# A radix-2 step of the transform over d, moved from TensorE to VectorE, ScalarE and GpSimd, with row- and column-tiled matmuls behind it

## The chip, the cores and the metric

One NeuronCore of a Trainium2 chip runs the whole kernel as one program. The metric is device time in microseconds (us), the median of three runs. Besides these there is one profiled execution, whose trace is the source of every duration below. Engines are named as in the profile: PE is TensorE's matmul stream and PEld its weight loads, DVE is VectorE, ACT ScalarE, POOL GpSimd, and SP is SyncE, whose queue issues all of this kernel's transfers.

## The reference

```python
x = A_x                                    # (1, 2048, 512) f32
xn = layernorm(x, axis=-1)
# A: spectral filter over both axes (S = 2048, D = 512)
X = rfft2(xn, axes=(-2, -1)) * (A_w_r + 1j * A_w_i)        # 2048 x 257
a = irfft2(X, s=(S, D), axes=(-2, -1))
# B: Dense -> Mish -> Dense, F = 1792
h = xn @ B_w1 + B_b1
b = (h * tanh(softplus(h))) @ B_w2
return x + a + b
```

Everything is f32 on input and output. On TensorE each f32 operand is written as a sum of two f16 numbers, high and low.

## The kernel before, in words

Two pieces of work share the engines. The MLP (B) is 56 tiles (4 row groups g by 14 blocks f of the hidden axis). Each tile is two half tiles: `mlp_up` (12 matmuls of 128x128 weights by 512 columns into `ph`, then Mish on ACT into `hb`, then a split of `hb` into high and low f16 halves `a`) and `mlp_down` (12 matmuls by 512 columns into `pa`). The helper `mm3` (lines 59 to 65) is the f16 pair product: high by high, high by low, low by high, three matmuls, each with its own weight load.

The spectral filter (A) is a chain of matrix products with DRAM between them, because each step needs another axis on the partitions:

- `s1_forward`, 16 units: transform over 128 values of the row axis, three matmuls of 512 columns into `psS`; ACT and DVE write the high and the low half of `y1`; two units are stored together to `d_y1`.
- `p2_unit`, 16 units (4 rounds c by 4 groups g): loads `yt` from `d_y1`; the remaining 16-point transform over rows, mixed with a radix-4 step over d; 12 matmuls with 128x128 weights (the data) and 128 moving columns (the constants) into `psP`; ACT and DVE write `z`.
- `spectrum`, 4 rounds: the rest of the transform over d. `dmm` makes the pairs `ere`/`eim` and `ore`/`oim`, each of 2 x 6 matmuls of 512 columns. DVE and POOL separate the even part into its components (`X`), multiply by the filter (tiles `wE`, `wO`, loaded in `p2_unit`), and combine (`w`, `o`). Row 0 goes a way of its own through small copies (`g0`, `r0`, `h0`). Each result is split into f16 halves in `u`.
- `dp_unit`, 16 units: inverse transform over d, 12 matmuls with weights `u` and 256 moving columns into `psA`; ACT and DVE write `at`, which is stored to `d_a`.
- `ip_unit`, 16 units: loads `ai` from `d_a`; three matmuls of 512 columns into `psT`; ACT and DVE write `tt`, stored to `d_t`.
- `s1_inverse`, 16 units: loads `yi` from `d_t`; three matmuls of 512 columns into `psY`; DVE adds the result to the MLP's output or to x.

Before them come the loading and scaling of the MLP's weights (`load_w1`, `w2_scale`, `split_w1`, `split_w2`), layernorm with transposes of the rows through TensorE (`norm`, tiles `xh`, `pt`, `xnT`), and the largest magnitude of the filter (`prep_spectral`).

The order is set at the end of the kernel function. `stream_a` is a generator over the spectral units from `p2_unit` to `ip_unit`; after each of its steps, as many half tiles of the MLP are emitted as keep pace with `B_END` = 100 of 112 half tiles over `N_UNITS` = 72 steps. The rest of the MLP is spread over the 16 `s1_inverse` units. The tile scheduler then fixes the order on each engine at build time: by priority in program order, but letting a later instruction go first where an earlier one isn't ready in its model. The first matmul of a spectral group is tied behind the previously emitted matmul (`keep_in_program_order`), so it can't move ahead of MLP work emitted before it, while later MLP work may move ahead of it. `issue_after` puts `w2_scale` behind the last DVE instruction of the first four `s1_forward` units.

Buffers that matter: the PSUM pool `ps_f` has two banks (tag "f"), used by `psS`, `psP`, the results of `dmm`, `psA`, `psT` and `psY`; `ps_h` has two, for `ph` and the transposes; `ps_a` has four, for the MLP's accumulators. In SBUF the tiles `z` and `u` have one buffer each, `at` and `tt` share three, `yt`, `ai`, `yi` and `xh` share four.

Of the kernel before, what the change touches and what calls it, by code (L numbers as in the profile page):

```python
# [19 lines left out]
P = 128  # L20
# [10 lines left out]
O_P2, O_IP2, O_DE, O_DO, O_IE, O_IO, O_ID = 0, 512, 1024, 2048, 3072, 4096, 5120  # L31
# [4 lines left out]
def spectral_mlp_kernel(ctx, tc, x, wt, w0, w1, b1, w2, cT, cIT, cM, out):  # L36
# [17 lines left out]

    d_y1 = dp.tile([64, P, 256], F16, tag="d_y1", name="d_y1")
# [15 lines left out]
    c_p2 = cMt[:, O_P2 : O_P2 + 512].rearrange("p (v h q) -> p v h q", v=2, h=2)  # L71
    c_ip2 = cMt[:, O_IP2 : O_IP2 + 512].rearrange("p (v h q) -> p v h q", v=2, h=2)
    c_de = cMt[:, O_DE : O_DE + 1024].rearrange("p (e o h q) -> p e o h q", e=2, o=2, h=2)
    c_do = cMt[:, O_DO : O_DO + 1024].rearrange("p (e o h q) -> p e o h q", e=2, o=2, h=2)
    c_ie = cMt[:, O_IE : O_IE + 1024].rearrange("p (e h q) -> p e h q", e=2, h=2)
    c_io = cMt[:, O_IO : O_IO + 1024].rearrange("p (e h q) -> p e h q", e=2, h=2)
# [14 lines left out]
    y1s = {}  # L91

    def s1_forward(g, s, xh):
        if True:
            s2 = 4 * g + s
            ps = ps_f.tile([P, D], F32, tag="f", name=f"psS1_{s2}")
            mm3(ps, lambda h: cTt[:, s2, h, :], lambda h: xh[:, h, :], True, True)
            if s % 2 == 0:
                y1s[0] = tp.tile([P, 2, 4, 2, P], F16, tag="X", name=f"y1_{s2}", bufs=2)
            y1v = y1s[0][:, s % 2]  # L100
            psv = ps.rearrange("p (a b) -> p a b", a=4)
# [4 lines left out]
            if s % 2 == 1:  # L106
                nc.sync.dma_start(
                    d_y1[4 * (s2 - 1) : 4 * (s2 + 1)].rearrange("a p e -> p a e"),
                    y1s[0].rearrange("p s a h e -> p (s a) (h e)"),
                )  # L110
        return last.ins
# [21 lines left out]
    def norm(g, ts):  # L133
# [14 lines left out]
        for s in range(4):  # L148
# [5 lines left out]
            if g == 0:  # L154
                xh = tp.tile([P, 2, D], F16, tag=f"w{s}", name=f"xh_{s2}")
            else:
                xh = qp.tile([P, 2, D], F16, tag="q1", name=f"xh_{s2}")
# [132 lines left out]
    def prep_spectral():  # L290
        mxw = sp.tile([P, 9], F32, tag="mxw", name="mxw")
        for c in range(8):
            t = big.tile([P, 1024], F32, tag="big", name=f"wm_{c}")
            nc.sync.dma_start(t, wt[:, c // 2, 1024 * (c % 2) : 1024 * (c % 2) + 1024])
            nc.vector.tensor_reduce(mxw[:, c : c + 1], t, axis=AX.X, op=ALU.max, apply_absolute_value=True)
            yield 1.1
# [11 lines left out]
        sc["u"] = scalars("u", pW, 2.0**-16, recip=True)  # L308
# [14 lines left out]
    def halves(t):  # L323
        v = t.rearrange("p (g a q) -> p a g q", g=4, a=2)
        return v[:, 0], v[:, 1]

    def flat(t):
        return t.rearrange("p a b -> p (a b)")

    zt, ut, wts = {}, {}, {}  # L330

    def p2_unit(c, g):
        if g == 0:
            wEt = big.tile([P, 2, 512], F32, tag="big", name=f"wE_{c}")
            nc.sync.dma_start(flat(wEt), wt[:, c, 0:1024])
            wOt = big.tile([P, 2, 512], F32, tag="big", name=f"wO_{c}")
            nc.sync.dma_start(flat(wOt), wt[:, c, 1024:2048])
            wts[c] = (wEt, wOt)
            zt[c] = tp.tile([P, 2, 4, 4, P], F16, tag="z", name=f"z_{c}")
        z = zt[c]  # L340
        if True:
            fg = 4 * c + g
            yt = qp.tile([P, 4, 2, P], F16, tag="q1", name=f"yt_{fg}")
            nc.sync.dma_start(
                yt.rearrange("p a h e -> p (a h e)"),
                d_y1.rearrange("a (c f) e -> (a c) (f e)", c=2)[:, fg * 1024 : (fg + 1) * 1024],
            )
            ps = ps_f.tile([P, 4, P], F32, tag="f", name=f"psP2_{fg}")
# [3 lines left out]
            psv = ps.rearrange("p l (k q) -> p k q l", k=4)  # L352
            zh = z[:, 0, :, g, :].rearrange("p k (q l) -> p k q l", l=4)
            zl = z[:, 1, :, g, :].rearrange("p k (q l) -> p k q l", l=4)
            nc.scalar.mul(zh, psv, 2.0**-14)
            nc.vector.scalar_tensor_tensor(zl, psv, 2.0**-14, zh, op0=ALU.mult, op1=ALU.subtract)

    def spectrum(c):
        s_u, c0t = sc["u"], sc["c0t"]
        z = zt[c]  # L360
        wEt, wOt = wts[c]
        u = tp.tile([P, 2, 4, 4, P], F16, tag="u", name=f"u_{c}")
        ut[c] = u

        def dmm(name, mat, k0, o):
            ps = ps_f.tile([P, 512], F32, tag="f", name=name)
            for e in range(2):
                mm3(
                    ps,
                    lambda h: mat[:, e, o, h, :],  # L370
                    lambda h: z[:, h, k0 + e].rearrange("p g q -> p (g q)"),
                    e == 0,
                    e == 1,
                    e == 0,
                )
            return ps

        def split_u(k, r):
            split(flat(u[:, 0, k]), flat(u[:, 1, k]), r, s_u)

        ere = dmm(f"ere_{c}", c_de, 0, 0)
        eim = dmm(f"eim_{c}", c_de, 0, 1)
        es = tp.tile([P, 512], F32, tag="xs", name=f"es_{c}", bufs=2)
        nc.scalar.copy(es, eim)

        er0 = tp.tile([1, 512], F32, tag="xs", name=f"er0_{c}", bufs=2)
        nc.scalar.copy(er0, ere[0:1, :])  # L387
        q0 = slice(32 * c, 32 * c + 4)
        g0 = sp.tile([P, 2, 2, 64], F32, tag="g0", name=f"g0_{c}")
        nc.sync.dma_start(  # L390
            g0[q0, 0].rearrange("g a q -> g (a q)"), er0.rearrange("p (g q) -> p g q", g=4)
        )
        nc.sync.dma_start(
            g0[q0, 1].rearrange("g a q -> g (a q)"), es[0:1].rearrange("p (g q) -> p g q", g=4)
        )
        r0 = sp.tile([P, 2, 2, 64], F32, tag="r0", name=f"r0_{c}")
        for a in range(2):
            m2 = sp.tile([P, 2, 64], F32, tag="m2", name=f"m2_{c}_{a}")
            nc.vector.tensor_mul(r0[q0, :, a, :], g0[q0, :, 0, :], c0t[q0, 2 * a])
            nc.vector.tensor_mul(m2[q0], g0[q0, :, 1, :], c0t[q0, 2 * a + 1])  # L400
            nc.vector.tensor_add(r0[q0, :, a, :], r0[q0, :, a, :], m2[q0])
# [9 lines left out]
        def xq(k):  # L411
            return X[:, k].rearrange("p (g q) -> p g q", g=4)
# [466 lines left out]
```

## Time and profile before

| | |
|---|---|
| median of 3 runs | 422.85 us (420.85 to 426.03) |
| profiled execution | 426.21 us |
| its span, first to last instruction | 424.4 us |
| mean granted TensorE clock | 0.986 of full |
| PE busy | 391.0 us, 2099 matmuls |
| DVE busy | 241.3 us, 453 instructions |
| ACT busy | 172.4 us, 261 instructions |
| POOL busy | 42.2 us, 45 instructions |
| DMA | 61.02 MB, mean 144 GB/s |

Times in the profile are those of the profiled execution. A row of a timeline gives the start and the duration in us, then engine, line of the kernel, operation, output and inputs with the buffer numbers left out, and shapes (for a matmul: weights, then moving operand); a bracket behind it is the idle time of its engine before it and what ended that. Matmul durations are modelled and overlap the next matmul; the distance from start to start is what a matmul costs in a stream. A row of a group of instructions gives total busy time and mean ns of one behind the bar, and a row for a tile gives the shortest, median and longest duration. A row of waits gives the total in us, the number of times and the longest one.

### The profile page before, as it was taken

Reading aid. Unit: us, or ns where it says so; the run is one execution under the profiler, and the core shown is the slowest. Engines: PE = TensorE matmul, PEld = TensorE weight load, DVE = VectorE, ACT = ScalarE, POOL = GpSimd, SP = SyncE. Lnnn points to the kernel's source line nnn. Section 1 sums busy time; section 2 is a strip of 40 time slices with the busy share of each in tenths; the row PEclk is TensorE's granted clock in tenths of the full one; section 3 lists DMA queues with packets and bytes.
Section 4 is the critical chain, followed back from the end, with each engine's and each line's share of the span. In section 5 each row is a group of like instructions: output and inputs, shape, how many; then the busy total and the mean of one; then the engine's idle time right before and its main releaser. Section 6 shows DMA issues by size and latency. Waiting matters only on the chain.

```text
span 424.4 us, 5542 instructions
## 1 busy us (share of the span) xinstructions
PE 391.0 (92%) x2099; PEld 194.1 (46%) x2099; DVE 241.3 (57%) x453; ACT 172.4 (41%) x261; POOL 42.2 (10%) x45
## 2 busy tenths in 40 slices
PE   0787899499899999989999999999999999999995
PEld 0433344244445455436554455554455544554442
DVE  5759899995455123773247943339625287332554
ACT  2896462442635324334343334333524243433110
POOL 0000102332040000220002020011200022000000
PEclk9999999889999999989999999999999999999999
DMA  7899882588154701032227214233024210233796
GB/s 247 268 345 330 272 259 91 159 256 269 53 160 114 233 25 51 0 99 71 81 76 239 85 49 123 76 127 124 2 74 151 74 51 25 76 127 126 219 296 247
DMA packets 48811, 61.02 MB, mean 144 GB/s; under 512 B 3168, under 2 KB 31360, under 8 KB 48528
## 3 DMA queue, kind: packets, MB, share of 16 engines
q1 hardware_dynamic: 48784, 60.67, 44.7%
q8 instruction: 16, 0.26, 0.2%
q14 instruction: 11, 0.09, 0.1%
HBM read 43.85 MB, written 16.78 MB: 143 GB/s over the span
## 4 chain that ended last, share of the span: by engine, by line
PE 72%; DVE 13%; DMA 6%; ACT 4%; issue 2%; POOL 0%; SPq 0%; DVEq 0%; ACTq 0%; POOLq 0%
PE pa L65 9%; PE pa L64 9%; PE pa L61 9%; PE ph L61 9%; PE ph L65 9%; PE ph L64 9%; DVE q L273 2%; DMA w1s<-in_w_dram 2%; PE pt L164 2%; ACT w1t L236 1%; PE psA L61 1%; PE psA L64 1%; PE psA L65 1%; DMA w2s<-in_w_dram 1%; DMA ai<-d_a 1%
## 5 line engine op out<-in xcount | busy, mean ns | idle before, releaser
L61 PE MATMUL ph<-xnT,w1t 128*128 128x512 f16 x224 | 85.2, 380 | 2.6 <-ACT hb L533 1.5
L533 ACT ACTIVATE hb<-ph,b1t,sc_exp 128x512 f32<-128x512 f32 x56 | 43.4, 775 | 107.4 <-PE ph L65 104.2
L65 PE MATMUL ph<-xnT,w1t 128*128 128x512 f16 x224 | 84.8, 379 | 2.4 <-DVE w1t L208 2.4
L61 PE MATMUL pa<-w2t,a 128*128 128x512 f16 x224 | 85.3, 383 | 1.6 <-ACT w2t L207 1.6
L64 PE MATMUL pa<-w2t,a 128*128 128x512 f16 x224 | 85.7, 383 | 0.3 <-DVE w2t L208 0.3
L65 PE MATMUL pa<-w2t,a 128*128 128x512 f16 x224 | 86.0, 384 | 0.0
L208 DVE SCALAR_TENSOR_TENSOR a<-hb,sc_a,a 128x512 f16<-128x512 f32 x56 | 42.3, 755 | 76.2 <-ACT a L207 76.1
L64 PE MATMUL ph<-xnT,w1t 128*128 128x512 f16 x224 | 85.0, 379 | 0.0
L207 ACT ACTIVATE a<-hb,sc_a 128x512 f16<-128x512 f32 x56 | 40.1, 719 | 2.2 <-PE pa L65 0.9
L65 PEld LDWEIGHTS <-w1t 128*128 128x128 f16 x224 | 21.9, 98 | 29.7 <-DVE w1t L208 3.4
L65 PEld LDWEIGHTS <-a 128*128 128x128 f16 x224 | 22.0, 98 | 27.4 <-issue 1.6
L64 PEld LDWEIGHTS <-w1t 128*128 128x128 f16 x224 | 21.9, 98 | 27.1 <-issue 2.3
L61 PEld LDWEIGHTS <-a 128*128 128x128 f16 x224 | 22.1, 99 | 26.5 <-issue 2.7
L61 PEld LDWEIGHTS <-w1t 128*128 128x128 f16 x224 | 21.9, 98 | 26.4 <-ACT w1t L207 1.6
L64 PEld LDWEIGHTS <-a 128*128 128x128 f16 x224 | 22.1, 99 | 25.2 <-issue 1.1
L164 PE MATMUL pt<-cMt,xh 128*128 128x128 f16 x128 | 12.3, 253 | 18.5 <-ACT xh L159 11.3
L487 DVE SCALAR_TENSOR_TENSOR at<-psA,at 128x512 f16<-128x512 f32 x16 | 11.0, 689 | 19.1 <-ACT at L486 19.1
L422 POOL TENSOR_TENSOR w<-X,wE 128x512 f32<-128x512 f32 x4 | 5.1, 1269 | 165.7 <-ACT er L387 76.8
L164 PEld LDWEIGHTS <-xh 128*128 128x128 f16 x128 | 10.3, 114 | 23.7 <-ACT xh L159 12.0
L509 DVE SCALAR_TENSOR_TENSOR tt<-psT,tt 128x512 f16<-128x512 f32 x16 | 11.0, 690 | 14.1 <-ACT tt L508 13.9
L160 POOL TENSOR_TENSOR xh<-xs,xh 128x512 f16<-128x512 f32 x12 | 14.4, 1216 | 45.2 <-ACT xh L159 29.9
L486 ACT ACTIVATE at<-psA 128x512 f16<-128x512 f32 x16 | 9.4, 589 | 22.8 <-PE psA L65 22.8
(150 smaller groups left out, 551.2 us busy)
## 6 DMA issues: line engine op xcount, KB each, us to landing
x<-in_x_dram SPq DMA_DIRECT2D x8, 512.0 KB
d_y<-y SPq DMA_DIRECT2D x8, 512.0 KB
wm<-in_wt_dram SPq DMA_DIRECT2D x8, 512.0 KB
yt<-d_y SPq DMA_DIRECT2D x16, 256.0 KB
d_a<-at SPq DMA_DIRECT2D x16, 256.0 KB
ai<-d_a SPq DMA_DIRECT2D x16, 256.0 KB
d_t<-tt SPq DMA_DIRECT2D x16, 256.0 KB
yi<-d_t SPq DMA_DIRECT2D x16, 256.0 KB
```

The costliest lines, as they stand in the source:

```text
L61: first = nc.tensor.matmul(ps, stat(0), mov(0), start=start, stop=False)
L64: nc.tensor.matmul(ps, stat(0), mov(1), start=False, stop=False)
L65: nc.tensor.matmul(ps, stat(1), mov(0), start=False, stop=stop)
L160: (nc.vector if g == 0 else nc.gpsimd).tensor_sub(xh[:, 1, :], xs, xh[:, 0, :])
L164: nc.tensor.transpose(pt[:, h, dc, :], xh[:, h, dc * P : (dc + 1) * P], ident)
L207: hi = nc.scalar.activation(dst_h, src, AF.Copy, scale=scale)
L208: nc.vector.scalar_tensor_tensor(dst_l, src, scale, dst_h, op0=ALU.mult, op1=ALU.subtract)
L273: nc.vector.tensor_reduce(q[:, c : c + 1], t, axis=AX.XY, op=ALU.max, apply_absolute_value=True)
L486: nc.scalar.mul(at[:, :, 0, :], ps, 2.0**-15)
L487: nc.vector.scalar_tensor_tensor(at[:, :, 1, :], ps, 2.0**-15, at[:, :, 0, :], op0=ALU.mult, op1=ALU.subtract)
L509: nc.vector.scalar_tensor_tensor(tt[:, :, 1, :], ps, 2.0**-12, tt[:, :, 0, :], op0=ALU.mult, op1=ALU.subtract)
L533: nc.scalar.activation(hb, ph, AF.Mish, bias=b1t[:, f : f + 1], scale=s_exp[k])
```

## The change

The first radix-2 step over d (rows a and a + 256 of the d axis) is done where `y1` is evicted: a new helper `butterfly` forms sum and difference of the two halves of the PSUM tile in f32, and splits the result into f16 halves with a copy on ACT and a subtraction on POOL. The same helper does the last radix-2 step of the inverse in `ip_unit`. `y1` is stored unit by unit.

The matrices behind it are halved. `p2_unit` issues 24 matmuls with 64 columns of weights, alternating between the lower and upper 64 output partitions (column tiles), so that one half of the partitions of `z` holds one half of the frequencies and the other half the rest. `d_pair` takes the place of `dmm`: 24 matmuls with 64 rows, alternating between the two halves of the rows (row tiles) into two PSUM banks. `product` takes the place of the multiplications by the filter; real and imaginary parts now lie in different partition halves. `load_wt` loads the filter inside `spectrum`, each piece twice, once for each half of the partitions. `dp_unit` keeps its 12 matmuls and moves 128 columns instead of 256; `ip_unit` has 6 matmuls of 256 columns instead of 3 of 512. `s1_inverse` reads its input in another order.

```diff
+    def butterfly(out, a, b, scale, name):
+        bc = tp.tile([P, 256], F32, tag="bc", name=f"bc_{name}", bufs=2)
+        nc.scalar.mul(bc, b, scale)
+        t = tp.tile([P, 4, 2, 64], F32, tag="bt", name=f"bt_{name}", bufs=2)
+        av = a.rearrange("p (k e) -> p k e", k=4)
+        bv = bc.rearrange("p (k e) -> p k e", k=4)
+        nc.vector.scalar_tensor_tensor(t[:, :, 0], av, scale, bv, op0=ALU.mult, op1=ALU.add)
+        last = nc.vector.scalar_tensor_tensor(t[:, :, 1], av, scale, bv, op0=ALU.mult, op1=ALU.subtract)
+        tv = t.rearrange("p k c e -> p k (c e)")
+        nc.scalar.copy(out[:, :, 0, :], tv)
+        nc.gpsimd.tensor_sub(out[:, :, 1, :], tv, out[:, :, 0, :])
+        return last.ins
...
     def s1_forward(g, s, xh):
-            nc.scalar.mul(y1v[:, :, 0, :], psv, 2.0**-17)
-            last = nc.vector.scalar_tensor_tensor(
-                y1v[:, :, 1, :], psv, 2.0**-17, y1v[:, :, 0, :], op0=ALU.mult, op1=ALU.subtract
-            )
+        y1 = tp.tile([P, 4, 2, P], F16, tag="q2", name=f"y1_{s2}", bufs=3)
+        last = butterfly(y1, ps[:, 0:256], ps[:, 256:512], 2.0**-17, f"s1_{s2}")
...
     def p2_unit(c, g):
-            for l in range(4):
-                v = 1 if fg == 0 and l == 0 else 0
-                mm3(ps[:, l, :], lambda h: yt[:, l, h, :], lambda h: c_p2[:, v, h, :], True, True, l == 0)
+        for pr in range(2):
+            for k in range(2):
+                for t, (hs, hm) in enumerate(((0, 0), (0, 1), (1, 0))):
+                    for be in range(2):
+                        v = int(fg == 0 and pr == 0 and be == 0)
+                        first = nc.tensor.matmul(
+                            ps[64 * be : 64 * be + 64, pr, k, :],
+                            yt[:, 2 * pr + be, hs, k, :],
+                            c_p2[:, k, v, hm, :],
+                            start=t == 0,
+                            stop=t == 2,
+                        )
...
+    def load_wt(c, be):
+        w = []
+        for ri in range(2):
+            t = big.tile([P, 4, 256], F32, tag="big", name=f"wt_{c}_{be}_{ri}")
+            at = 1024 * (4 * c + 2 * be + ri)
+            for h in range(2):
+                nc.sync.dma_start(t[64 * h : 64 * h + 64].rearrange("p k q -> p (k q)"), wt[:, at : at + 1024])
+            w.append(t)
+        wts[c, be] = w
...
+    def d_pair(c, k0):
+        z = zt[c]
+        ps = [ps_f.tile([P, 2, 256], F32, tag="f", name=f"psD_{c}_{k0}_{be}") for be in range(2)]
+        for k in range(2):
+            for e in range(2):
+                for t, (hs, hm) in enumerate(((0, 0), (0, 1), (1, 0))):
+                    for be in range(2):
+                        rows = slice(64 * be, 64 * be + 64)
+                        first = nc.tensor.matmul(
+                            ps[be][:, k],
+                            c_d[rows, k0 + k, e, hs, :],
+                            z[rows, hm, 2 * (k0 + k) + e].rearrange("p g q -> p (g q)"),
+                            start=e == 0 and t == 0,
+                            stop=e == 1 and t == 2,
+                        )
...
+    def product(r, x, w, k, name):
+        wre, wim = w[0][:, k], w[1][:, k]
+        t2 = tp.tile([P, 2, 256], F32, tag="t2", name=f"t2_{name}", bufs=2)[:, 0 : k.stop - k.start]
+        nc.vector.tensor_mul(r, x, wre)
+        nc.vector.scalar_tensor_tensor(
+            t2[0:64], x[64:128], -1.0, wim[64:128], op0=ALU.mult, op1=ALU.mult
+        )
+        nc.vector.tensor_mul(t2[64:128], x[0:64], wim[0:64])
+        nc.gpsimd.tensor_add(r, r, t2)
...
     def spectrum(c):
+        ab = d_pair(c, 0)
+        xa, es = [], []
+        for be in range(2):
+            load_wt(c, be)
+            e = tp.tile([P, 256], F32, tag="es", name=f"es_{c}_{be}", bufs=2)
+            nc.scalar.copy(e, ab[be][:, 0])
+            for r in range(2):
+                nc.sync.dma_start(
+                    g0[q0, r, be].rearrange("g a q -> g (a q)"),
+                    e[64 * r : 64 * r + 1].rearrange("p (g q) -> p g q", g=4),
+                )
+            ea, eb = halves(e)
+            nc.scalar.mul(jbv[0:64], eb[64:128], -1.0)
+            nc.scalar.copy(jbv[64:128], eb[0:64])
+            nc.vector.tensor_add(xp, ea, jbv)
+            nc.vector.tensor_sub(xm, ea, jbv)
...
+            yield 1.6
...
+        for be in range(2):
+            w = wts[c, be]
+            r = tp.tile([P, 2, 256], F32, tag="r", name=f"r_{c}_{be}", bufs=2)
+            product(r[:, 1:2], ab[be][:, 1:2], w, slice(1, 2), f"b_{c}_{be}")
+            ra = tp.tile([P, 1, 256], F32, tag="ra", name=f"ra_{c}_{be}", bufs=2)
+            product(ra, xa[be], w, slice(0, 1), f"a_{c}_{be}")
+            rp, rm = halves(ra[:, 0])
+            ua, ub = halves(r[:, 0])
+            nc.vector.tensor_add(ua, rp, rm)
+            nc.vector.tensor_sub(ub[0:64], rp[64:128], rm[64:128])
+            nc.vector.tensor_sub(ub[64:128], rm[0:64], rp[0:64])
...
+            split_u(0, be, r)
+            yield 2.0
...
+        cd = d_pair(c, 2)
+        for be in range(2):
+            r = tp.tile([P, 2, 256], F32, tag="r", name=f"r2_{c}_{be}", bufs=2)
+            product(r, cd[be], wts[c, be], slice(2, 4), f"c_{c}_{be}")
+            split_u(2, be, r)
+            yield 2.0
...
     def dp_unit(c, g):
-            for k, m in ((0, c_ie), (2, c_io)):
-                pk = flat(ps[:, k : k + 2])
-                for e in range(2):
-                    mm3(pk, lambda h: u[:, h, k + e, g, :], lambda h: m[:, e, h, :], e == 0, e == 1, k == 0 and e == 0)
+        for k in range(4):
+            mm3(
+                ps[:, k % 2, :, k // 2, :],
+                lambda h: u[:, h, k, g].rearrange("p q r b -> p (q r b)"),
+                lambda h: c_id[:, k, h, :].rearrange("p (e d) -> p e d", e=2),
+                True,
+                True,
+                k == 0,
+            )
...
     def ip_unit(c, g):
-                mm3(ps, lambda h: c_ip2[:, 0, h, :], lambda h: ai[:, :, h, :], True, True, True)
+        for k in range(2):
+            parts = [(1, slice(0, 1)), (0, slice(1, 4))] if fg == 0 else [(0, slice(0, 4))]
+            for n, (v, ls) in enumerate(parts):
+                mm3(
+                    ps[:, k, ls],
+                    lambda h: c_ip2[:, k, v, h, :],
+                    lambda h: ai[:, ls, h, k, :],
+                    True,
+                    True,
+                    k == 0 and n == 0,
+                )
+        butterfly(tt, ps[:, 0].rearrange("p l e -> p (l e)"), ps[:, 1].rearrange("p l e -> p (l e)"), 2.0**-12, f"t_{fg}")
```

The constant matrices and the layout of the filter in DRAM are prepared to match; the two constant blocks have the size they had.

More of the change, by code (lines that the diff above doesn't have):

```diff
@@ L378, in split_u @@
[L378 to L389, printed above, removed]
@@ L390, in spectrum, with split_u, halves @@
-        nc.sync.dma_start(
-            g0[q0, 0].rearrange("g a q -> g (a q)"), er0.rearrange("p (g q) -> p g q", g=4)
+        def split_u(k, be, r):
+            v = u[:, :, k : k + 2, :, :, :, be].rearrange("p h k g q r -> p h (k g q r)")
+            split(v[:, 0], v[:, 1], flat(r), s_u)
+        def halves(t):
+            v = t.rearrange("p (g a q) -> p a g q", g=4, a=2)
+            return v[:, 0], v[:, 1]
+        q0 = slice(32 * c, 32 * c + 4)
+        g0 = sp.tile([P, 2, 2, 2, 32], F32, tag="g0", name=f"g0_{c}")
@@ new lines, in spectrum, with ordered, weights @@
+        r0 = sp.tile([P, 2, 2, 32, 2], F32, tag="r0", name=f"r0_{c}")
+        for a in range(2):
+            m2 = sp.tile([P, 2, 32, 2], F32, tag="m2", name=f"m2_{c}_{a}")
+            def ordered(t):
+                return t.rearrange("p r q b -> p r b q")
+            def weights(t):
+                return t.rearrange("p r (b q) -> p r b q", b=2)
+            nc.vector.tensor_mul(ordered(r0[q0, :, a]), g0[q0, :, :, 0], weights(c0t[q0, 2 * a]))
+            nc.vector.tensor_mul(ordered(m2[q0]), g0[q0, :, :, 1], weights(c0t[q0, 2 * a + 1]))
+            nc.vector.tensor_add(r0[q0, :, a], r0[q0, :, a], m2[q0])
```

420 lines of the change are left out of this document (172 added, 248 removed).

## The prediction

> **What bounds the kernel now.** The profile page comes first: who is busy, when, and what the chain that ended last is made of.
>
> ```profile
> span 424.4 us, 5542 instructions
> PE 391.0 (92%) x2099; PEld 194.1 (46%) x2099; DVE 241.3 (57%) x453; ACT 172.4 (41%) x261; POOL 42.2 (10%) x45
> PE   0787899499899999989999999999999999999995
> PE 72%; DVE 13%; DMA 6%; ACT 4%; issue 2%; POOL 0%; SPq 0%; DVEq 0%; ACTq 0%; POOLq 0%
> ```
>
> TensorE is busy for 391.0 of 424.4 us, and its free time lies in the first quarter of the slices. The stage windows (PE, PEld, DVE, ACT, POOL busy, then the granted clock) and TensorE's own list of waits say it more exactly.
>
> ```profile
> 172.00:195.00 23.00, 20.95 (x104) 9.86 (x103) 17.64 (x40) 8.31 (x12) 5.44 (x4) 0.93 0.15 47
> 195.00:386.70 191.70, 191.30 (x1077) 99.18 (x1076) 96.52 (x162) 73.95 (x114) 16.32 (x12) 1.00 0.29 94
> 386.70:420.10 33.40, 33.22 (x154) 14.84 (x152) 16.76 (x25) 5.10 (x7) 0.00 (x0) 1.00 0.73 232
> ...
> PE pt L164 <- ACT xh L159: 11.3, 1, 11.3
> PE pt L164 <- ACT xnT L166: 6.6, 2, 5.6
> ...
> PE oim L61 <- DVE w L450: 2.1, 1, 2.1
> ```
>
> From 195 us to 420 us TensorE has 0.6 us of idle time. The spectral stream runs in there, from about 155 us on, mixed with the MLP, and it shows one wait of note: 2.1 us in the first round of the spectrum. So TensorE work taken out of the stream shortens the kernel one for one, as long as the stream's chain through VectorE, GpSimd and DRAM doesn't become longer than the MLP matmuls that cover it. The other engines have room: DVE stands at 96.5 of 191.7 us there, POOL at 16.3.
>
> **TensorE, matrix by matrix.** Durations of matmuls in the trace are modelled ends; what counts is start to start. The TensorE timeline has it:
>
> ```profile
> 155.50 0.22 PE L61 MATMUL psP<-cMt,yt 128*128 128x128 f16 x1
> 155.55 0.22 PE L64 MATMUL psP<-cMt,yt 128*128 128x128 f16 x1
> ...
> 156.17 0.38 PE L61 MATMUL ph<-xnT,w1t 128*128 128x512 f16 x1
> ...
> 168.54 0.38 PE L61 MATMUL ere<-z,cMt 128*128 128x512 f16 x1
> ...
> 171.13 0.38 PE L61 MATMUL ph<-xnT,w1t 128*128 128x512 f16 x1
> ...
> 193.82 0.27 PE L61 MATMUL psA<-cMt,u 128*128 128x256 f16 x1
> ...
> 195.13 0.38 PE L61 MATMUL ph<-xnT,w1t 128*128 128x512 f16 x1
> ...
> 374.56 0.38 PE L61 MATMUL psT<-ai,cMt 128*128 128x512 f16 x1
> ...
> 375.20 0.38 PE L61 MATMUL ph<-xnT,w1t 128*128 128x512 f16 x1
> ```
>
> Twelve matmuls of 128 columns (p2) take 156.17 − 155.50 = 0.67 us, 0.056 each, and each of them has its own weight load. Twelve of 256 columns (dp) take 1.31 us, 0.109 each; twelve of 512 columns (ere and eim) 2.59 us, 0.216 each; the three of ip 0.64 us. So a full-array matmul costs its columns, and a new weight load with every matmul costs nothing down to 128 columns.
>
> (1) dp_unit, 16 times. It keeps 12 matmuls with 128x128 weights, and the moving side falls from 256 to 128 columns. That is the shape of p2 now: 1.31 − 0.67 = 0.64 us, times 16: **−10.2 us**. It uses no tiling, so this is the firmest term.
>
> (2) The transform over d, four rounds of two pairs. Now 2.59 us a pair. After: d_pair issues 24 matmuls of 64 rows by 256 columns, alternating between the two row halves. If the halves run side by side, that is 12 slots of 0.109 = 1.31 us and the saving is 1.28 × 8 = 10.2 us; if they run one behind the other, 24 × 0.109 = 2.62 us and nothing is saved (+0.3). A side-by-side pair needs two weight loads of 128 columns in 0.109 us, and the p2 rows show a load and a matmul every 0.056 us. So nothing that the trace shows forbids it, and I take **−10.2 us**, with +0.3 as the other end.
>
> (3) p2_unit, 16 times. 12 matmuls become 24, each with 64 columns of weights, alternating between column halves. Side by side: 12 slots of 0.056, no change. One behind the other: 24 × 0.056 = 1.34 us, +0.67 × 16 = +10.7 us. Here a full overlap needs a load and a matmul every 0.028 us, and the shortest pitch in the trace is 0.056; on the other hand a load has half the columns. I take the middle, **+5.3 us**, and keep both ends.
>
> (4) ip_unit: 3 matmuls of 512 become 6 of 256: 0.657 against 0.64, +0.3 us over 16. The strided reads of ip and s1_inverse still run 64 elements on end; I cost them at nothing.
>
> (5) Changes of tiling. 8 + 16 = 24 groups of tiled matmuls stand between full-array ones, so there are 48 changes. The trace has none. At the least a change is free: 128-, 256- and 512-column groups follow each other above without a gap. At the most TensorE has to run empty:
>
> ```profile
> L61 PE MATMUL psP<-cMt,yt 128*128 128x128 f16 x64 | 11.5, 219 | 0.0
> ```
>
> 219 ns of modelled length less the 56 ns of pitch leaves 163 ns in flight; 48 × 0.163 = 7.8 us. I take one matmul slot, 56 ns, each: **+2.7 us**.
>
> [...]
>
> **The other engines.** butterfly, 32 times, replaces one ACT and one DVE pass over 512 columns by a half ACT pass, two half DVE passes, a full ACT pass and a full POOL pass.
>
> ```profile
> L508 ACT ACTIVATE tt<-psT 128x512 f16<-128x512 f32 x16 | 9.5, 595 | 19.4 <-PE psT L65 19.2
> L509 DVE SCALAR_TENSOR_TENSOR tt<-psT,tt 128x512 f16<-128x512 f32 x16 | 11.0, 690 | 14.1 <-ACT tt L508 13.9
> L414 DVE TENSOR_TENSOR X<-ere,es 128x256 f32<-128x256 f32 x4 | 1.7, 422 | 9.5 <-ACT er L387 9.5
> L469 POOL TENSOR_TENSOR o<-o,o 128x512 f32<-128x512 f32 x4 | 5.1, 1266 | 50.0 <-DVE o L467 50.0
> ```
>
> DVE: 2 × 0.42 − 0.69 = +0.15 us; ACT about +0.4 (between nothing and the 0.595 of a full pass); POOL +1.27. Over 32 units that is +5, +13 and +41 us. In the spectrum the products change from two-engine multiplies to three DVE passes and one POOL pass each, some of them over half the rows; counted with 0.42 us for 256 columns and 0.69 for 512 this is an estimate of +8 us on DVE over the four rounds and nothing on POOL. In total DVE about 254, ACT 186, POOL 82 of 424 us: none becomes the bound, and after 155 us all of it lies beside TensorE. Without that cover a butterfly would cost its added latency, 0.4 + 0.15 + 1.27 = 1.8 us, before its store can start.
>
> The place without cover is the start: up to 82 us TensorE waits for ACT and DVE. Four butterflies run there, and w2_scale's reductions are queued on DVE behind the last of them. They add 4 × 0.15 us on DVE and 4 × 0.4 on ACT; POOL's passes slow DVE besides (below). I take **+1.5 us**, between 0 and 4.
>
> On SP's queue, 40 more transfers are issued: y1 is stored in 16 pieces, not 8, wt is loaded in 32 pieces of 64 rows, not 8 of 128, and g0 by 16 small copies, not 8. The queue keeps order, and stores already stand in it waiting for DVE:
>
> ```profile
> SPq L491 <- DVE at L487: 72.0, 16, 11.1
> SPq L107 <- DVE xnT L165: 14.0, 2, 12.4
> ```
>
> A y1 or tt store now waits for POOL too, and a loading of wt, yt or ai behind it comes 1.8 us later. TensorE had MLP matmuls in hand through such waits of 11 us, so I take **+1 us** for all stalls in the stream; the ends are −3.7 (the present stall goes away) and the rival below.
>
> **The sum.** −10.2 − 10.2 + 5.3 + 0.3 + 2.7 + 1.5 + 1.0 = −9.6 us. The profiled execution took 426.21 us (424.4 of span), which is 3.4 above the median of 422.85. 426.2 − 9.6 = 416.6; off the median the same saving gives **413 us**. A row-by-row spread for this case alone is 408 to 419.
>
> **The rivals.** *Full gain.* Column tiles overlap, changes of tiling are free: −10.2 − 10.2 + 0.3 + 1 = −19.1, say 403 us. For it: load and matmul follow at the array's pace in every row. Against: p2 would need twice the shown rate.
>
> *The tiling eats its gain.* d_pair overlaps, p2 doesn't (+10.7) and each change empties the array (+7.8): −10.2 − 10.2 + 0.3 + 10.7 + 7.8 + 2.5 = +0.9, 424 us. [...] For it: 0.056 us is the shortest pitch seen.
>
> *It doesn't do what it says.* The tiles never run side by side: (2) +0.3, (3) +10.7, with the rest −10.2 + 0.3 + 2.7 + 2.5 gives +6.3, 429 us. For it: no row of the trace has two matmuls in the array at once. Against: operands, weights and PSUM banks of the halves are disjoint.
>
> *Stalls of the spectrum: slower.* d_pair(c, 0) holds both buffers of the pool "f" until VectorE has read the products out of it, and ip_unit and d_pair(c, 2) need those buffers. The products run beside more POOL work, which stretches DVE:
>
> ```profile
> L421 DVE TENSOR_TENSOR w<-X,wE x4: 774/1346/1380, 173.8 to 343.2; 128x512 f32<-128x512 f32 x4
> L423 DVE TENSOR_TENSOR w<-X,wE x4: 692/1754/1754, 175.0 to 345.9; 128x512 f32<-128x512 f32 x4
> ...
> 182.84 0.38 PE L61 MATMUL oim<-z,cMt 128*128 128x512 f16 x1 [2.05 <-DVE w L450]
> ...
> 184.24 0.63 PE L65 MATMUL pa<-w2t,a 128*128 128x512 f16 x1
> 184.66 0.63 PE L61 MATMUL pa<-w2t,a 128*128 128x512 f16 x1
> ...
> 187.54 0.38 PE L64 MATMUL pa<-w2t,a 128*128 128x512 f16 x1
> ```
>
> A pass of 0.69 us takes 1.35 to 1.75 beside POOL, and the one present stall cost 2.05 us of idle time and then 3.3 us at a pitch of 0.42, half the clock: 1.6 more, 3.7 in all. Cover between the two pairs is four steps of some 0.8 half tile of 2.6 us, about 8.6 us. The chain is two e copies and six product passes of 0.42 us, 3.3 us plain, but up to 6 beside POOL and 11 with the small row-0 passes (2.7) and the two ip evictions ahead of it. Where it passes 8.6 us TensorE waits: by 2.5 us a pair, with 1.6 us of clock 4.1. At all eight pairs that is 33, less 9.6, or +23 (446 us); at five of them +11 (434); I take 440 us. It decides from an excess of about 1 us at every pair. Against it: MLP matmuls may be issued ahead of late spectral ones (only the first matmul of a group is tied, and only backwards), and 33 us of TensorE work lies behind the last ip unit.
>
> **How the numbers follow.** Forecast 0.38; full gain 0.22; tiling eats its gain 0.16; no overlap 0.08; stalls 0.16. Two per cent is 8.5 us, about what a measurement of this kernel can tell from no change: 414.4 and 431.3 are the marks. Faster: 0.22 and six tenths of the forecast, 0.46. Slower: the stalls and a third of no overlap, 0.19. The rest, 0.35, lies within 2%. The range from 401 to 431 holds the forecast, nearly all of the full gain and most of the flat cases; the bounds of (2), (3) and (5) reach as far.
>
> **What would show it.** Right: psA groups last 0.67 us; in d_pair two matmuls start within a few ns of each other and a pair of its groups takes about 1.3 us; p2 groups 0.67 to 1.34 us; gaps of some 0.05 us around tiled groups; TensorE busy near 380 us with no new wait of over 2 us after 155 us. Wrong: d_pair groups at 2.6 us (no overlap), p2 groups above 1.34 us, or TensorE waiting for DVE or for a buffer of "f" in each round with half clock behind it.

## The result, and the profile after

The changed kernel takes 447.22 us (445.65 to 450.57) against 424.44 us (420.85 to 426.07): 1.056 times the time before, with a 95% interval of 1.046 to 1.066. It is slower by 22.8 us; 413 us was forecast, and the range ended at 431.

The page of the changed kernel: span, busy times, TensorE by slices, its clock, and the chain that ended last.

```profile
span 443.9 us, 6516 instructions
PE 385.1 (87%) x2438; PEld 190.2 (43%) x2438; DVE 268.6 (61%) x529; ACT 188.8 (43%) x309; POOL 82.7 (19%) x85
PE   0784599939989999987998979999699996899996
PEclk9996689979999999999999999999999998999999
PE 16%; DVE 6%; DMA 2%; ACT 2%; issue 1%; POOL 0%; DVEq 0%; ACTq 0%; SPq 0%; POOLq 0%
```

PE's busy time fell by 5.9 us, and the span grew by 19.5: time was lost in waiting. PE's digits show it twice. At the start a run of low slices has a clock of 0.6 under it, and after 155 us, where a 9 stood in nearly every slice before, there are now 6, 7 and 8. The chain adds up to 27% of the span; it breaks off far from the start, and nothing is read from it here. The stage windows of the changed kernel, with the columns as in the prediction:

```profile
20.00:50.00 30.00, 18.72 (x67) 7.12 (x68) 22.88 (x36) 18.96 (x28) 6.42 (x5) 0.82 0.73 237
50.00:82.00 32.00, 29.54 (x124) 12.61 (x122) 25.40 (x62) 15.01 (x18) 2.90 (x4) 0.90 0.61 193
82.00:110.00 28.00, 21.31 (x115) 10.79 (x114) 24.63 (x48) 13.71 (x25) 12.22 (x11) 0.88 0.62 187
195.00:400.00 205.00, 187.95 (x1399) 99.15 (x1396) 125.96 (x231) 87.22 (x149) 40.81 (x38) 0.99 0.39 114
```

The same windows of the kernel before:

```profile
20.00:50.00 30.00, 23.61 (x105) 10.08 (x106) 23.67 (x41) 22.33 (x31) 1.78 (x2) 1.00 0.95 321
50.00:82.00 32.00, 26.52 (x135) 12.32 (x133) 30.52 (x77) 13.91 (x20) 4.88 (x4) 0.99 0.56 174
82.00:110.00 28.00, 27.43 (x138) 13.45 (x138) 18.98 (x29) 12.19 (x20) 7.51 (x13) 0.89 0.71 226
195.00:400.00 205.00, 204.60 (x1139) 105.23 (x1138) 101.64 (x169) 77.43 (x119) 16.32 (x12) 1.00 0.31 98
```

PE's busy time times its clock tells how much work a window got done. From 20 to 110 us that is 18.72 × 0.82 + 29.54 × 0.90 + 21.31 × 0.88 = 60.7 us after, and 74.3 before: the start is 13.6 us behind. In the stream, from 195 to 400 us, TensorE stands idle for 17 us, where before it was 0.4. TensorE's waits in the changed kernel, first the three rows up to 155 us that grew (they were 1.1, 1.5 and 1.6 us), then those behind it (waited for: us in total, times, longest):

```profile
PE ph L62 <- ACT w1t L209: 6.4, 2, 5.1
PE ph L62 <- ACT hb L557: 5.1, 2, 4.0
PE pa L62 <- ACT w2t L209: 2.5, 1, 2.5
...
PE psA L62 <- ACT u L209: 4.9, 4, 3.4
PE psP L358 <- DVE t_c L401: 3.3, 3, 1.3
PE psD L382 <- DVE t_b L401: 2.4, 2, 1.8
PE psA L66 <- DVE u L210: 2.3, 4, 0.7
PE psP L358 <- DVE z L371: 2.3, 3, 1.5
PE psT L62 <- DVE t_b L401: 1.8, 3, 0.9
```

Two losses, then. At the start TensorE waits for weights of the MLP and for its Mish (`hb`), which the change doesn't touch. In the stream it waits some 25 times for a short while, 19.7 us in all with three smaller rows, for `u`, `z` or a bank that the products still read. Before, the waits after 155 us were 2.4 us.

The TensorE groups themselves, in the changed kernel's timeline:

```profile
169.13 0.38 PE L66 MATMUL pa<-w2t,a 128*128 128x512 f16 x1
169.44 0.86 PE L358 MATMUL psP<-cMt,yt 128*64 128x128 f16 x24
170.23 0.39 PE L62 MATMUL ph<-xnT,w1t 128*128 128x512 f16 x1
...
183.08 0.38 PE L66 MATMUL pa<-w2t,a 128*128 128x512 f16 x1
183.39 1.48 PE L382 MATMUL psD<-z,cMt 64*128 64x256 f16 x24
184.81 0.39 PE L62 MATMUL ph<-xnT,w1t 128*128 128x512 f16 x1
```

The 24 column-tiled matmuls of p2 take 170.23 − 169.44 = 0.79 us, 33 ns each; the 24 row-tiled ones of `d_pair` take 1.42 us, where the pair took 2.59. Ahead of each group lies 0.31 us from the start of a matmul of 0.216: a gap of 0.09 us. In both, the two matmuls of a pair start 3 to 4 ns apart. So the tiles do run side by side, and what remains of a change of tiling is 0.09 us before the group and 0.11 to 0.12 in it (0.79 − 0.67, 1.42 − 1.31).

### The profile page after: what moved, and what is told of

Its sections match the earlier page's. It is cut to its first block, busy times and chain, and to the rows that moved or that the text cites. A ratio compares the mean times of both kernels' runs of the same rounds, so it can differ in the third digit from the quotient of the medians.

```text
span 443.9 us, 6516 instructions
## 1 busy us (share of the span) xinstructions
PE 385.1 (87%) x2438; PEld 190.2 (43%) x2438; DVE 268.6 (61%) x529; ACT 188.8 (43%) x309; POOL 82.7 (19%) x85
## 5 line engine op out<-in xcount | busy, mean ns | idle before, releaser
L62 PE MATMUL ph<-xnT,w1t 128*128 128x512 f16 x224 | 88.0, 393 | 12.4 <-ACT w1t L209 6.4
L66 PE MATMUL ph<-xnT,w1t 128*128 128x512 f16 x224 | 87.5, 391 | 0.6 <-DVE cl_H L177 0.3
L65 PE MATMUL ph<-xnT,w1t 128*128 128x512 f16 x224 | 87.5, 390 | 0.0
L210 DVE SCALAR_TENSOR_TENSOR a<-hb,sc_a,a 128x512 f16<-128x512 f32 x56 | 43.6, 781 | 62.5 <-ACT a L209 62.4
L101 POOL TENSOR_TENSOR tt<-bt_t,tt 128x512 f16<-128x512 f32 x16 | 18.9, 1180 | 105.0 <-ACT tt L100 69.6
L62 PEld LDWEIGHTS <-w1t 128*128 128x128 f16 x224 | 22.4, 100 | 33.2 <-ACT w1t L209 7.4
L65 PEld LDWEIGHTS <-w1t 128*128 128x128 f16 x224 | 22.4, 100 | 31.3 <-issue 9.4
L66 PEld LDWEIGHTS <-w1t 128*128 128x128 f16 x224 | 22.4, 100 | 29.5 <-issue 2.8
L209 ACT ACTIVATE u<-r,sc_u 128x512 f16<-128x512 f32 x16 | 13.9, 868 | 41.1 <-POOL r L402 18.8
L166 PE MATMUL pt<-cMt,xh 128*128 128x128 f16 x128 | 11.8, 245 | 18.0 <-ACT xh L161 11.2
L101 POOL TENSOR_TENSOR y<-bt_s,y 128x512 f16<-128x512 f32 x16 | 20.1, 1264 | 27.0 <-ACT y L100 11.4
L210 DVE SCALAR_TENSOR_TENSOR u<-r,sc_u,u 128x512 f16<-128x512 f32 x16 | 17.9, 1117 | 4.6 <-ACT u L209 4.5
```

The lines of the kernel that those rows point to most:

```text
L62: first = nc.tensor.matmul(ps, stat(0), mov(0), start=start, stop=False)
L65: nc.tensor.matmul(ps, stat(0), mov(1), start=False, stop=False)
L66: nc.tensor.matmul(ps, stat(1), mov(0), start=False, stop=stop)
L101: nc.gpsimd.tensor_sub(out[:, :, 1, :], tv, out[:, :, 0, :])
L166: nc.tensor.transpose(pt[:, h, dc, :], xh[:, h, dc * P : (dc + 1) * P], ident)
L209: hi = nc.scalar.activation(dst_h, src, AF.Copy, scale=scale)
```

## The start: experiments on GpSimd's queue

The POOL timeline of the changed kernel from 24 to 56 us (start, duration, [idle before, and what ended it]):

```profile
24.34 2.26 POOL L101 TENSOR_TENSOR y<-bt_s,y 128x512 f16<-128x512 f32 x2 [7.49 <-ACT w1t L238]
33.76 0.46 POOL L193 PARTITION_ALL_REDUCE qs_w<-qw  x1 [7.16 <-issue]
42.16 3.69 POOL L101 TENSOR_TENSOR y<-bt_s,y 128x512 f16<-128x512 f32 x2 [7.94 <-ACT w1t L209]
53.11 0.38 POOL L279 PARTITION_ALL_REDUCE qa<-qm  x1 [7.26 <-issue]
```

And of the kernel before:

```profile
26.93 0.46 POOL L191 PARTITION_ALL_REDUCE qs_w<-qw  x1 [9.80 <-ACT w1t L236]
43.27 1.32 POOL L277 PARTITION_ALL_REDUCE qa<-qm  x1 [15.89 <-DVE qm L275]
```

GpSimd also takes the maximum over partitions from which the scales of the MLP's weights come (`qs_w` for the second part of w1, `qa` for w2). Before, no other work lay between these in this stretch. Now the low halves of `y1` do, and each time GpSimd turns from subtraction to `PARTITION_ALL_REDUCE` it stands for 7 us with nothing to wait for ("issue"). The turn back costs about as much: the two rows of subtractions stand behind 7.49 and 7.94 us of idle time, which the profile puts down to ACT. For the first of them ACT had written the input by 18.21 us, 6.1 us before it starts. The reductions come 6.8 and 9.8 us later. Behind the first stands ACT, which can't scale w1 without `sc_w`; its row in the changed kernel:

```profile
36.64 5.32 ACT L209 ACTIVATE w1t<-w1s,sc_w 128x1024 f16<-128x1024 f32 x5 [5.64 <-DVE sc_w L187]
```

TensorE's row follows, 5.07 us of idle time and then a pitch of 0.40 us where the stream has 0.216 (the granted clock from 37.8 to 42 us is 0.50):

```profile
37.85 0.61 PE L62 MATMUL ph<-xnT,w1t 128*128 128x512 f16 x1 [5.07 <-ACT w1t L209]
38.25 0.63 PE L65 MATMUL ph<-xnT,w1t 128*128 128x512 f16 x1
```

What GpSimd does in the 7.16 and 7.26 us of the two "issue" rows, no row here shows.

**x1: the four early low halves on VectorE.**

```diff
+        low = (low or nc.gpsimd).tensor_sub(out[:, :, 1, :], tv, out[:, :, 0, :])
...
+        last = butterfly(y1, ps[:, 0:256], ps[:, 256:512], 2.0**-17, f"s1_{s2}", nc.vector if g == 0 else None)
```

> The changed kernel, with the subtraction of the first four butterflies (s1_forward, g = 0) on DVE, not POOL. Theory A: at the start the POOL subtractions stand between partition_all_reduce calls, and each change between the two kinds costs POOL some 7 us (idle rows of 7.2 to 7.9 us before qs_w, qa and y in the changed kernel); so the scale of w1 and of w2 comes late and TensorE waits (5.1 and 4.0 us). Then these waits go, sc_w comes near 28.5 us as before the change, and the kernel gains 8 to 14 us: 433 to 439. Rival B: the start is slower because of the added ACT and DVE passes and the stores of y1; then moving 4 x 0.7 us onto DVE gains nothing: 446 to 450.

Measured: 432.71 us, 1.015 [1.008, 1.023]. Against the kernel before, measured beside it (425.22), that is +7.5 us in place of +22.8: GpSimd's part at the start is worth about 15 us (the intervals leave some 5 us either way). Its POOL rows:

```profile
27.11 0.46 POOL L193 PARTITION_ALL_REDUCE qs_w<-qw  x1 [10.21 <-ACT w1t L238]
36.24 1.32 POOL L279 PARTITION_ALL_REDUCE qa<-qm  x1 [8.68 <-DVE qm L277]
```

**x2: the kernel before, with tiny GpSimd subtractions.** One column of `y1` is subtracted after each of the first four evictions, into a tile that nobody reads. It has the turn of work on GpSimd and none of the passes.

```diff
+            if g == 0:
+                dm = sp.tile([P, 1], F32, tag="dm", name=f"dm_{s2}", bufs=4)
+                nc.gpsimd.tensor_sub(dm, y1v[:, 0, 0, 0:1], y1v[:, 0, 1, 0:1])
```

> The kernel before, with one subtraction of 128x1 elements on POOL added behind each of the first four evictions of s1_forward into a scratch tile that nobody reads. It is under 0.2 us of work each. Theory A (each change between tensor operations and partition_all_reduce costs POOL about 7 us): qs_w of the second part of w1 comes some 5 to 7 us later than at 26.9 us, and the kernel takes 430 to 437. Rival B (only the amount of work counts): within 1 us of the kernel before.

Measured: 429.97 us, 1.012 [1.007, 1.016], +4.8 us, at the lower edge of the mechanism's forecast. POOL in x2:

```profile
23.73 0.47 POOL L108 TENSOR_TENSOR dm<-y 128x1 f32<-128x1 f16 x3 [6.86 <-DVE w1t L211]
34.46 0.46 POOL L194 PARTITION_ALL_REDUCE qs_w<-qw  x1 [10.26 <-issue]
...
50.41 0.38 POOL L280 PARTITION_ALL_REDUCE qa<-qm  x1 [8.30 <-issue]
```

Three passes of 0.47 us together, and behind them 10.26 us of idle time. ACT's last pass over w1, which the reduction needs, ends at 26.65 us (26.84 in the kernel before); so 2.4 us of the 10.26 are the input's, and 7.8 us are the turn's. The turn costs, not the work. The reductions stand 7.5 and 7.1 us later than before.

**x10: x1 with the same tiny subtractions.** This puts the turn alone back into the changed kernel (low halves on VectorE, as in x1).

```diff
+        if g == 0:
+            dm = sp.tile([P, 1], F32, tag="dm", name=f"dm_{s2}", bufs=4)
+            nc.gpsimd.tensor_sub(dm, y1[:, 0, 0, 0:1], y1[:, 0, 1, 0:1])
```

> The kernel of x1 (low half of the first four units on DVE) with one POOL subtraction of 128x1 elements added behind each of them, as in x2. POOL's sequence of kinds is then that of the changed kernel, but y1 and the buffers bt no longer wait for POOL. If the late scales of w1 and w2 are the whole loss at the start, 443 to 448. If a good part of it came through buffers and stores that waited for POOL's subtraction, it is 436 to 441, nearer to x1's 432.7, like the 5 us that x2 cost.

Measured: 444.22 us, 1.042 [1.038, 1.047], +18.1 us against +7.5 for x1. So the turn of GpSimd's work by itself costs 10.6 us, of the 15 us that GpSimd's part is worth. The other 4.7 us are barely clear of the intervals (1.038 to 1.047 here, 1.046 to 1.066 with the full passes), and that the full passes make them is not shown. Here `qa` stands at 49.70 against 36.24 in x1, 13.5 us later, where in x2 it was 7.1 later than in the kernel before; that fits the larger price here. The two kernels also wait in different places: x10 has one wait of 6.6 us of `psS` for `bt_s` at 88 us, which neither the changed kernel nor x1 has. Why the kernel before absorbs so much more was not settled.

**x7: the first four units later, GpSimd kept.** The four `s1_forward` are emitted behind the last split of w2, so that no reduction stands behind them. Made on x3, below.

```diff
-    for n in range(4):
-        last_dve = s1_forward(0, n, xhs[n])
...
     split_w2(6)
+    for n in range(4):
+        s1_forward(0, n, xhs[n])
```

> The changed kernel with pacing by weights as in x3, and the first four s1_forward units moved from before w2_scale to behind the last split_w2, tied to that place on TensorE; their low halves stay on POOL. No tensor operation of POOL stands between the first four partition_all_reduce calls any more, and the start has 4 x 1.5 us less of DVE work. Theory A: the start is at least as fast as in x4, 417 to 424. If the loss at the start had come from the added work alone, wherever it runs, it would return at the new place: 428 to 434.

Measured: 426.44 us, 1.004 [1.001, 1.008]: 8.2 us better than x3, where x4 below gains 11.4 over x3, and a little above its forecast. The reductions are in time (25.32 and 34.53 us), but the next layer norm's transposes are later than they were (6.6 us of this wait in the kernel before). The row of x7's waits:

```profile
PE pt L166 <- ACT xnT L168: 10.8, 2, 9.8
```

## The stream: experiments on cover

How much MLP work stands beside a unit of the stream is set by counting steps. A round of the spectrum has six steps now; it had seven. (By its code the kernel before has 76 steps in all and not 72, so its half tiles of the stream are used up at the 72nd; the changed kernel has 72.) Of `N_UNITS` = 72 it thus gets 8.3% of the half tiles in place of 9.7, and VectorE's part of the round has grown: between 195 and 400 us it is busy 126.0 us, against 101.6. In one round VectorE runs without a gap of note from about 239 to 254 us, and again from 256 on. Its timeline in the changed kernel, where a matmul group of p2 waits behind the products:

```profile
257.87 0.69 DVE L398 SCALAR_TENSOR_TENSOR t_c<-psD,wt 64x512 f32<-64x512 f32 x1
258.57 0.68 DVE L401 TENSOR_TENSOR t_c<-psD,wt 64x512 f32<-64x512 f32 x1
```

The matching TensorE row:

```profile
259.40 0.86 PE L358 MATMUL psP<-cMt,yt 128*64 128x128 f16 x24 [1.33 <-DVE t_c L401]
```

The group can have its bank when the last product of `d_pair` has been read out, at 258.57 + 0.68 us, and it starts 0.15 us after.

**x3: the same kernel, paced by the weights of the steps.** `stream_a` already yields a weight for each step (1.6 or 2.0 in the spectrum, 0.7 to 1.0 elsewhere, 84.8 in all), and the loop that emits the MLP ignores it. By weight a round gets 11.2 of 84.8, 13.2%.

```diff
-N_UNITS = 72
+N_UNITS = 84.8
...
-    for _ in stream_a():
-        used += 1
+    for wgt in stream_a():
+        used += wgt
```

> The changed kernel, with the half tiles of the MLP spread by the weights that stream_a yields (1.6 and 2.0 for steps of the spectrum, 0.7 to 1.0 for the others, 84.8 in all) and not evenly over 72 steps: more MLP work lies between the dependent steps of the spectrum, less between the others. Theory C: the some 20 us of waits in the stream come because the spectrum's chain on DVE is longer than the MLP work emitted beside it; then they fall below 10 us and the kernel takes 433 to 440. Rival D: the waits come from the two PSUM banks of the pool f and from a DVE that is full there, whatever the pace: 444 to 450.

Measured: 434.44 us, 1.021 [1.014, 1.028], +9.2 us in place of +22.8. TensorE's waits after 155 us in x3, all of them:

```profile
PE psT L62 <- DMA ai<-d_a: 2.7, 3, 1.5
PE psY L62 <- DMA yi<-d_t: 1.2, 2, 0.9
PE psP L358 <- DVE z L371: 0.9, 2, 0.6
PE psA L62 <- ACT u L209: 0.6, 1, 0.6
PE psA L66 <- DVE u L210: 0.5, 1, 0.5
```

That is 5.9 us in place of 19.7: 13.8 us of waits gone, 13.6 us of time. Not one instruction was changed, only how much MLP work stands between the steps.

**x9: the kernel before, with the same pacing**, as a control (the edit is that of x3).

> The control to x3: the kernel before, with its MLP half tiles spread by the weights that stream_a yields (84.8 in all there too). Its stream has one wait of 2.1 us with 1.7 us of half clock behind it. Theory C (the pacing pays where the spectrum's chain outgrows its cover, which only the change brings): 421 to 427, no difference. If the pacing is simply better for any kernel of this kind, 412 to 418.

Measured: 426.81 us, 1.003 [0.999, 1.007]: no difference. Of these two kernels, pacing helps only the one whose spectrum the change made too long for its cover.

**x6: the products' sums on VectorE.** Is it GpSimd's passes, stretching VectorE's? All sums of `product` go to VectorE.

```diff
-        nc.gpsimd.tensor_add(r, r, t2)
+        nc.vector.tensor_add(r, r, t2)
```

> The changed kernel, with the addition at the end of each product on DVE, not POOL. It takes 8 us of POOL work a round away and puts 3 x 0.42 + 2 x 0.69 or so onto DVE. Theory E (POOL beside DVE stretches DVE's passes, the split of u above all, 1.12 us where it is 0.80 alone, and that makes the stalls): the split of u falls to about 0.85, the stream's waits on TensorE fall by a third or more, 438 to 443. Rival C alone (the chain is longer than the MLP work emitted beside it, by its number of steps): the waits change by less than 5 us, 443 to 450.

Measured: 448.26 us, 1.056 [1.049, 1.063], as the changed kernel. The split of `u` by groups, in the changed kernel:

```profile
L210 DVE SCALAR_TENSOR_TENSOR u<-r,sc_u,u 128x512 f16<-128x512 f32 x16 | 17.9, 1117 | 4.6 <-ACT u L209 4.5
```

and in x6:

```profile
L210 DVE SCALAR_TENSOR_TENSOR u<-r,sc_u,u 128x512 f16<-128x512 f32 x16 | 12.8, 799 | 5.2 <-ACT u L209 5.0
```

The stretching is real, 1117 ns against 799, but taking it away and paying for it with more VectorE passes changes nothing: TensorE's waits after 155 us are 19.8 us in place of 19.7. VectorE as a whole is busy for 271.2 us in place of 268.6, so the run shows that moving the sums doesn't help; what the stretching alone costs it can't show.

**x4: x1 and x3 together.**

> Both edits together. If A and C hold, they add up: 420 to 430. If only A: 433 to 439. If neither: 446 to 450.

Measured: 422.98 us, 0.994 [0.991, 0.998], −2.2 us. The parts alone gave back 15.3 and 13.6 us, together 25.0 of 28.9: nearly additive, so they are two causes and not one seen twice. The new order also has a price. In x3 and x4 alike, three of the eight `d_pair` groups are split: the scheduler puts the 12 matmuls of one half first, then other work, then the 12 of the other half. The first of the three in x4:

```profile
219.58 1.48 PE L382 MATMUL psD<-z,cMt 64*128 64x256 f16 x12
...
221.99 1.47 PE L382 MATMUL psD<-z,cMt 64*128 64x256 f16 x12
```

Each half takes 1.41 us by itself (work follows the first at 221.00 us), so these three groups run nothing side by side and cost about 4 us in all.

**x8: x4 with `B_END` = 104**, four half tiles more beside the stream.

> The kernel of x4 with B_END = 104 instead of 100: more of the MLP's half tiles are emitted beside the spectral stream, fewer behind it. If the waits left in x4's stream (some 10 us: ai, psA, psP, m) are still a lack of cover, it gains 1 to 5 us: 418 to 422. If the MLP work is then missing behind the last ip unit, it loses as much: 424 to 428.

Measured: 424.89 us, 0.997 [0.994, 1.000]. No gain: TensorE's waits after 155 us are 7.8 us, where x4 has 5.5, so more MLP work beside the stream doesn't take away what is left in x4.

**x5: x4 without alternation.** In `p2_unit` and `d_pair` the loop over `be` goes outermost: the same 24 matmuls in the same tiles, but first all of one half, then all of the other.

```diff
-        for k in range(2):
-            for e in range(2):
-                for t, (hs, hm) in enumerate(((0, 0), (0, 1), (1, 0))):
-                    for be in range(2):
+        for be in range(2):
+            for k in range(2):
+                for e in range(2):
+                    for t, (hs, hm) in enumerate(((0, 0), (0, 1), (1, 0))):
```

> The kernel of x4 (low half on DVE at the start, pacing by weights), with the loop over be moved outermost in p2_unit and d_pair, so that all matmuls of one half of the array are issued before those of the other. The same 24 matmuls, in another order. If the alternation is what lets two tiles run side by side, p2 groups go from 0.79 to about 1.45 us and d_pair groups from 1.42 to about 2.7: 16 x 0.66 + 8 x 1.3 = 21 us more TensorE work, and the kernel takes 438 to 446. If the two halves overlap by themselves or not at all, it stays at 421 to 425.

Measured: 429.05 us, 1.010 [1.006, 1.014], 5.9 us above x4. The groups in x5:

```profile
163.34 1.33 PE L358 MATMUL psP<-cMt,yt 128*64 128x128 f16 x24
164.61 0.39 PE L62 MATMUL ph<-xnT,w1t 128*128 128x512 f16 x1
...
184.25 2.37 PE L382 MATMUL psD<-z,cMt 64*128 64x256 f16 x24
186.56 0.39 PE L62 MATMUL ph<-xnT,w1t 128*128 128x512 f16 x1
```

1.27 us in place of 0.79, and 2.31 in place of 1.42: the overlap comes from the order. One half behind the other in full would be 24 × 0.056 = 1.34 and 24 × 0.109 = 2.62 us; the rows stay a little below that, and around the middle of a group some matmuls of the two halves still alternate in the trace (in `d_pair` with starts 8 to 20 ns apart). Since three of the `d_pair` groups ran one half after the other in x4 too (two times 1.41 us, in x5 as well), the edit adds 16 × 0.48 + 5 × 0.89 = 12.1 us of work, yet 5.9 us of time; my forecast was too high. In the profiled executions the waits after 155 us fell from 5.5 to 3.0 us and the mean clock rose from 0.980 to 0.991; that these took up the other half is likely, but not shown.

**x11: x7 with the four low halves on VectorE.**

> The kernel of x7 with the low halves of the four moved units on DVE (x4 with these units behind the last split_w2). The start is free of butterflies, and no tensor operation of POOL comes before the fifth all-reduce but the layernorm's own. If x7's waits of the transposes on xnT (9.8 us at 83 us, 3.4 at 117) come from POOL's queue, it takes 417 to 422, below x4's 423; if they come from DVE being full there, 425 to 430.

Measured: 423.43 us, 0.992 [0.990, 0.994]. That lies between its two forecasts: TensorE still waits 7.9 us for `xnT` (10.8 in x7), so whether GpSimd's queue or a full VectorE makes that wait stays open. x4 and x11 are both faster than the kernel before, by less than 1%; between these two the runs don't tell.

## Why the prediction was wrong, step by step

*Terms (1) to (5), TensorE: right, and together too cautious.* dp's matmuls follow at 0.056 us, as forecast: −10.2. `d_pair` with its gap is 1.42 + 0.09 against 2.59: −8.6 over eight. p2 with its gap is 0.79 + 0.09 against 0.67: +3.4 over sixteen. ip is 0.65 against 0.64: +0.2. The sum is −15.2 where the terms were −12.1. The changes of tiling are in it: about 0.2 us for a group, 4.9 us for the 24, above the +2.7 taken and below the 7.8 estimated for an array run empty. Column tiles overlap in full, which the middle value of term (3) didn't expect; that was a choice between two ends and not a reading. The sign named for being right, two matmuls of a pair starting within a few ns, came (3 to 4 ns); the other one, no new wait of over 2 us after 155 us, did not (3.4 us for `u`). With its load, a matmul of p2 takes 33 ns.

*Term "start", +1.5 (0 to 4): this step failed.* It counted the new passes on ACT and VectorE, and asked what is queued behind them on VectorE. It didn't ask that of GpSimd, whose two reductions scale the MLP's weights. The price, about 15 us by x1, is for the most part not that of the passes (x2, x10) but of a turn between two kinds of work on one engine. The kernel before had a row that shows the turn, the other way round, where a layer norm's pass follows a reduction:

```profile
117.36 2.27 POOL L160 TENSOR_TENSOR xh<-xs,xh 128x512 f16<-128x512 f32 x2 [7.08 <-issue]
```

The prediction didn't read it. That the added GpSimd work lies beside TensorE was an argument from the share of busy time.

*Term "stalls", +1: this step failed, and the slower rival named its place.* The spectrum's chain did outgrow its cover and the price was 13.6 us by x3. But the rival had it as one wait of 2.5 us at each pair, for a buffer of "f" at `d_pair` and ip; the rows show only 2.4 us there for `psD` and 1.8 for `psT`, and 12.8 us at dp and p2, in waits of up to 3.4 us. Two reasons can be read off: VectorE's added work was sized at +13 us and is +27.3 (268.6 − 241.3), and I counted the steps between the two pairs, which stay four, and not those behind the second pair, which fall from three to two. How much of the 13.6 us each of the two makes was not measured.

*The sum.* TensorE's −15.2 and the measured +22.8 leave 38 us for what was costed at +2.5. x4 gives back 25 of them. Of the 13 that stay in x4, its waits after 155 us are 5.5 us, against 2.4 before, and PE's work between 110 and 155 us is about 4 us behind (41.55 us at a clock of 0.96, against 43.58 at 1.00; 2.7 us of it is one wait of `pa` for VectorE's `m`). The three split `d_pair` groups are about 4 us more, for which term (2) had no place. That leaves some 2 us that were not located.

*The rivals and the range.* The rival on the slower side stood at 440 us, 27 above the forecast. It had the right stage, but twice the price that x3 shows (13.6 us); that the measured 447 lies nearer to it than to the forecast is luck, for about half of the loss is at the start, and for that there was no rival at all. The range ended at 431, below that rival by itself. Three small slips changed nothing: four steps of 0.8 half tile of 2.6 us are 8.3 us and not 8.6, 422.85 − 19.1 is 404 and not 403, and the chance of "faster" adds up to 0.45 and not 0.46.

## What to carry to other kernels

Before work is put on an engine that looks free, read what else stands in its queue and who waits for it: here 10% busy hid two reductions on which the larger part of w1 and all of w2 hang. A kernel whose order is paced by a count of steps has to be paced anew when a change shortens one engine's part of a step and lengthens another's; a gain on the bounding engine is worth only as much as the other engines can keep up with (here 13.6 us of TensorE's time in the stream came back with the pacing of x3). Tiled matmuls on disjoint halves ran side by side here when they were issued in turn (0.79 and 1.42 us a group, against 1.27 and 2.31 in x5), and the trace shows whether the scheduler left them so: in x4 it didn't for three groups of eight.

## What the runs showed of the hardware

- GpSimd stands idle for 7.1 to 10.3 us between an elementwise pass and a following `PARTITION_ALL_REDUCE` ("issue" in the changed kernel, x2 and x10), whatever the size of the pass: 0.47 us of passes in x2 had the longest. Counted from when the input is ready, too, it is 7.0 and 7.3 us in the changed kernel and 7.8 us for the first one in x2. The other way round, from a reduction to a pass, the kernel before shows 7.08 us.
- Two column tiles of 64 weights and 128 moving columns, issued in turn, run at 33 ns a matmul with a load each (0.79 us for 24, changed kernel); one half behind the other, in x5, at 53 ns (1.27 us). Two row tiles of 256 columns: 59 ns in turn (1.42 us for 24, changed kernel), 96 ns in x5 (2.31 us), and 1.41 us for the 12 of one half alone in x4.
- A change of tiling costs about 0.2 us for a group there and back (changed kernel: 0.09 us ahead of the group and 0.11 to 0.12 in it), where the estimate of 163 ns in flight each way (219 ns of modelled length less 56 of pitch, in the kernel before) would have been 0.33.
